# DMA transposes for Q and x in place of TensorE transposes, with a reordered start, in a linear-attention plus ELU-MLP kernel

## The chip, the cores and the metric

One core of a Trainium2 chip. The time is the device time of one execution in microseconds (us); smaller is better. Each kernel was run several times, and a run is called fast or slow by its time and its granted TensorE clock; only fast runs enter the verdicts. PE is TensorE (PEld its weight loads), DVE VectorE, ACT ScalarE, POOL GpSimd, SP SyncE. "L360" is line 360 of the kernel in question; the changed kernel has other line numbers than the kernel before, so the same matmul is L318 in one and L347 in the other.

## The reference, cut to what matters

```python
# q, k, v: (8, 8, 576, 64) float32;  g_norm: (64,)
kv  = einsum('bhsd,bhse->bhde', k, v)            # 64x64 for each batch and head
out = einsum('bhsd,bhde->bhse', q, kv)
rms = sqrt(mean(out * out, axis=-1, keepdims=True) + 1e-06)
x   = (out / rms * g_norm)                       # then heads side by side: (4608, 512)
h   = x @ w_in                                   # w_in  (512, 2048)
g   = where(h > 0, h, exp(minimum(h, 0)) - 1)    # ELU
return (g @ w_out).astype(float32)               # w_out (2048, 512)
```

Of the kernel before, what the change touches and what calls it, by code (L numbers as in the profile page):

```python
# [9 lines left out]
BF16 = mybir.dt.bfloat16  # L10
AF = mybir.ActivationFunctionType
ALU = mybir.AluOpType
# [4 lines left out]
def kernel(  # L17
# [13 lines left out]
    nc = tc.nc  # L31
# [6 lines left out]
    J = 4  # L38
# [2 lines left out]
    KC = DM // P  # L41
    FC = DF // P
    NT = B + 1

    const = ctx.enter_context(tc.tile_pool(name="const", bufs=1))
    stage = ctx.enter_context(tc.tile_pool(name="stage", bufs=1))
# [61 lines left out]
    def fetch(b, eng=nc.sync):  # L108
        fetch_q(b, eng)
        for name, src in (("k", k), ("v", v)):  # L110
            out_, in_ = fetch_kv(name, src, b)
            eng.dma_start(out=out_, in_=in_)  # L112

    def load_w_in(s):
        cols = slice(s * 512, s * 512 + 512)
        nc.gpsimd.dma_start(
            out=w_in_sb[:, :, cols], in_=moe_w_in.rearrange("(c p) f -> p c f", p=P)[:, :, cols]
        )

    def load_w_out(s):  # L120
        fs = slice(4 * s, 4 * s + 4)
        nc.gpsimd.dma_start(
            out=w_out_sb[:, fs, :], in_=moe_w_out.rearrange("(c p) f -> p c f", p=P)[:, fs, :]
        )
# [56 lines left out]
    def se_mm(T, j, qT, se_ps):  # L181

        ov = se_ps.rearrange("p (u l s e) -> p u l s e", u=2, l=2, s=2)
        for p in range(NPAIR):
            s, u = p // 2, p % 2
            if T < B:
                nc.tensor.matmul(  # L187
                    ov[:, u, :, s, :],
                    lhsT=qT[:, p, j * P : j * P + P],
                    rhs=bd_kv[:, T, p, :],  # L190
                    start=True,
                    stop=True,
                )
            else:
                for l in range(2):
                    nc.tensor.matmul(
                        ov[l * 64 : l * 64 + 64, u, :, s, :],
                        lhsT=qT[:, p, j * P + l * 64 : j * P + l * 64 + 64],
                        rhs=bd_kv[:, 2 * j + l, p, :],
                        start=True,  # L200
                        stop=True,
                    )
# [25 lines left out]
    def attention(T):  # L228
        st = {}

        def kv():
            if T == B:
                return
            kv_ps = at_tile(FP32)
            for u in range(2):
                kv_mm(T, [kv_ps[:, 0:512], kv_ps[:, 512:1024]], u)
            kv_v = kv_ps.rearrange("p (s x e) -> p s x e", s=2, e=P)[:, :, 0:2, :]
            bd_v = bd_kv[:, T].rearrange("p (s u) e -> p s u e", s=2)
            for l in range(2):
                ls = slice(l * 64, l * 64 + 64)  # L240
                nc.scalar.copy(bd_v[ls, :, :, ls], kv_v[ls, :, :, ls])

        def q_t():
            qt_ps = at_tile(BF16).rearrange("p (r t) -> p r t", r=NPAIR)
            for p in range(NPAIR):
                q_t_mm(bf["q", T], qt_ps, p)
            qT = attp.tile([P, NPAIR, G], BF16, name="qT", tag="qT")
            st["qT"] = qT
            nc.vector.tensor_copy(out=qT[:, 0:2, :], in_=qt_ps[:, 0:2, :])  # L249
            nc.scalar.copy(qT[:, 2:4, :], qt_ps[:, 2:4, :])  # L250

        def se(h):


            def product():
                se_ps = at_tile(FP32).rearrange("p (c f) -> p c f", c=2)
                for c in range(2):
                    se_mm(T, 2 * h + c, st["qT"], se_ps[:, c, :])
                st["se", h] = se_ps
                st["sq", h] = square(se_ps, 2)  # L260

            def sums():
                st["ss", h] = sum_heads(st.pop(("sq", h)), 2)

            def inv():
                inv_rms(st["ss", h])

            def scale():
                if h == 0:
                    st["xs"] = attp.tile([P, J, DM], BF16, name="xs", tag="xs")  # L270
                rows = st["xs"][:, 2 * h : 2 * h + 2, :]
                scale_rows(rows, st.pop(("se", h)), st.pop(("ss", h)), 2)

            return product, sums, inv, scale

        def x_t():
            xs = st["xs"]
            xt_ps = at_tile(BF16).rearrange("p (r t) -> p r t", r=NPAIR)
            for c in range(KC):
                for j in range(J):  # L280
                    nc.tensor.transpose(  # L281
                        xt_ps[:, c, j * P : j * P + P],
                        xs[:, j, c * P : c * P + P],
                        ident,
                    )
            x = attp.tile([P, KC, G], BF16, name="xT", tag="xT")
            xT[T] = x
            nc.vector.tensor_scalar(  # L288
                out=x[:, 0:2, :], in0=xt_ps[:, 0:2, :], scalar1=g_col, scalar2=None, op0=ALU.mult
            )  # L290
            nc.scalar.mul(x[:, 2:4, :], xt_ps[:, 2:4, :], g_col)  # L291

        pieces = {"kv": kv, "q": q_t, "x": x_t}
        for h in range(2):
            for name, piece in zip(("se", "sum", "inv", "mul"), se(h)):
                pieces[f"{name}{h}"] = piece
        return pieces
# [4 lines left out]
    def mm1(T, i, cols=(slice(0, 512),), relu=False, spare=False):  # L302
# [11 lines left out]
        for cs in cols:  # L314
            for a in range(2):
                f = 2 * i + a
                for c in range(KC):
                    nc.tensor.matmul(  # L318
                        h_ps[a][:, cs],
                        lhsT=w_in_sb[:, c, f * P : f * P + P],  # L320
                        rhs=x[:, c, cs],
                        start=(c == 0),
                        stop=(c == KC - 1),
                    )
# [49 lines left out]
    def mm2_half(T, i):  # L374
        mm2(T, i // 2, 8 * (i % 2), 8 * (i % 2) + 8)
# [82 lines left out]
    se_at = at_tile(FP32)  # L458
    se_ps += [se_at[:, 0:512], se_at[:, 512:1024]]
    for j in range(J):  # L460
        se_mm(0, j, qT0, se_ps[j])
    idle(10)
    xs0 = attp.tile([P, J, DM], BF16, name="xs", tag="xs")
    x0 = attp.tile([P, KC, G], BF16, name="xT", tag="xT")
    xT[0] = x0
    xt_ps = ps_m1.tile([P, 2, G], FP32, name="xt_ps", tag="mm1").rearrange(
        "p a t -> p (a t)"
    ).bitcast(BF16).rearrange("p (a r c t) -> p a r c t", a=2, r=2, c=KC)
# [47 lines left out]
            cast_kv("v", b, Q)  # L516

    fetch(1)
    for s in range(2):
        load_w_in(s)  # L520
    cast_q(1, Q)
    for s in range(2, 4):
        load_w_in(s)
    cast_kv("k", 1, Q)
    cast_kv("v", 1, Q)
    for s in range(4):
        load_w_out(s)

    def first_products(T, at, second, start, relu=(), spare=()):


        early, late = {}, {}
        for name, i in start.items():
            late.setdefault(i, []).append(name)
            if name in ("se0", "se1"):
                early.setdefault(i + 1, []).extend(("sum" + name[2], "inv" + name[2]))
                late.setdefault(i + 1, []).append("mul" + name[2])
        for i in range(9 if 8 in early else 8):
            if i == 8:
                for name in early[8] + late[8]:  # L540
                    at[name]()
                break
            cols = (slice(0, 256), slice(256, 512)) if T == 0 and i == 0 else (slice(0, 512),)
            rest = mm1(T, i, cols, i in relu, i in spare)
            for name in early.get(i, ()):
                at[name]()
            if i in second:
                second[i]()
            rest()
            for name in late.get(i, ()):  # L550
                at[name]()

    at = attention(1)
    at["fetch"] = lambda: fetch(2, nc.scalar)
    start = {"q": 1, "kv": 4, "se0": 5, "fetch": 6, "se1": 7}
    first_products(0, at, {}, start, (1, 3, 5, 7), (2, 5))
    mm2_half(0, 0)
    mm2_half(0, 1)
    at["x"]()
    mm2_half(0, 2)  # L560

    cast_all(2)
    fetch(3)
    at = attention(2)
    second = {i: (lambda i=i: mm2_quarter(0, 6 + i)) for i in range(8)}
    start = {"q": 1, "kv": 2, "se0": 3, "se1": 5, "x": 7}
    first_products(1, at, second, start, (1, 3, 5, 7))
    mm2_half(0, 7)

    for T in range(2, NT):  # L570
        second = {i: (lambda i=i: mm2_half(T - 1, i)) for i in range(8)}
        at, start = None, {}
        if T + 1 < NT:
            at, start = attention(T + 1), {"kv": 0, "q": 1, "se0": 2, "se1": 4, "x": 6}
            cast_all(T + 1)
        if T + 2 < B:
            fetch(T + 2)
        elif T + 2 == B:
            fetch_q(B)
        first_products(T, at, second, start)  # L580
    for i in range(8):
        mm2_half(NT - 1, i)

# [29 lines left out]
```

## The kernel before: the parts that the change and the argument touch

The 4608 tokens are worked in nine groups of 512. Groups 0 to 7 are the first 512 tokens of each batch, group 8 is the 64 left over from each. For a group the two MLP products are 64 matmuls each, 128x128 by 128x512. The attention of group T+1 is cut into small pieces, placed between the products of group T:

```python
def attention(T):
    def kv():                        # K^T V of the batch: 36 small matmuls, then two ScalarE copies
        ...
    def q_t():                       # Q must lie with head_dim on the partitions
        qt_ps = at_tile(BF16)...     # the one PSUM tile of the attention
        for p in range(NPAIR):
            q_t_mm(bf["q", T], qt_ps, p)                            # 16 TensorE transposes
        nc.vector.tensor_copy(out=qT[:, 0:2, :], in_=qt_ps[:, 0:2, :])
        nc.scalar.copy(qT[:, 2:4, :], qt_ps[:, 2:4, :])
    def se(h):                       # scores of half a group; square, sum, 1/rms, scale -> xs
        ...
    def x_t():                       # x must lie with d_model on the partitions
        for c in range(KC):
            for j in range(J):
                nc.tensor.transpose(xt_ps[:, c, j*P:j*P+P], xs[:, j, c*P:c*P+P], ident)
        nc.vector.tensor_scalar(out=x[:, 0:2, :], in0=xt_ps[:, 0:2, :], scalar1=g_col, ...)
        nc.scalar.mul(x[:, 2:4, :], xt_ps[:, 2:4, :], g_col)        # g_norm on the way out of PSUM
```

The steady loop, and the start (the attention of group 0 is done alone first, up to about 22 us):

```python
    fetch(1)                                   # Q, K, V of batch 1, SyncE
    for s in range(2):    load_w_in(s)         # weights: GpSimd, cast to bf16 on the way
    cast_q(1, Q)                               # GpSimd, waits for Q of batch 1
    for s in range(2, 4): load_w_in(s)
    cast_kv("k", 1, Q); cast_kv("v", 1, Q)
    for s in range(4):    load_w_out(s)
    ...
    at["fetch"] = lambda: fetch(2, nc.scalar)  # batch 2: issued by ScalarE inside group 0
    start = {"q": 1, "kv": 4, "se0": 5, "fetch": 6, "se1": 7}
    ...
    for T in range(2, NT):
        second = {i: (lambda i=i: mm2_half(T - 1, i)) for i in range(8)}
        if T + 1 < NT:
            at, start = attention(T + 1), {"kv": 0, "q": 1, "se0": 2, "se1": 4, "x": 6}
            cast_all(T + 1)
        if T + 2 < B: fetch(T + 2)
        ...
        first_products(T, at, second, start)
```

`first_products` issues eight steps; step i is an eighth of group T's first product, its ELU, an eighth of group T-1's second product, and the pieces whose number in `start` is i. A tuple such as (1, 3, 5, 7) after `start` names its Relu steps: there ScalarE also writes relu(h) to SBUF, and VectorE's last ELU operation, which then need not read PSUM, takes 0.69 us and not 1.22 in the start.

## Time and profile before

| | before |
|---|---|
| time, median of 4 runs | 320.69 us (320.2 to 321.54) |
| span of the profiled run | 317.4 us |
| PE busy | 299.1 us (94%) |
| first product of group 2 starts | 81.94 us |
| period of a steady group | 31.52 us |

The profiled run took 319.24 us; it is a fast run, but not one of the four, and it is 1.45 us below their median.

The chain of waits runs back from the last instruction; its line by engine, from the page of the kernel before:

```profile
PE 80%; DMA 8%; DVE 4%; ACT 4%; ACTq 1%; POOL 0%; issue 0%; SPq 0%; DVEq 0%
```

The windows view of the kernel before, over two steady groups. Columns: the stretch; its length and PE busy time with the number of instructions; then PEld, DVE, ACT, POOL; granted clock; DMA share; GB/s.

```profile
117.10:148.60 31.50, 31.50 (x213) 16.12 (x212) 19.47 (x23) 16.05 (x22) 7.97 (x14) 1.00 0.41 142
148.60:180.10 31.50, 31.50 (x213) 16.13 (x212) 20.17 (x23) 16.05 (x22) 8.12 (x14) 1.00 0.40 142
```

PE is busy for the whole of each stretch at full clock, while VectorE and ScalarE have a third to a half of it free. So in the steady part only PE's own work counts. Its timeline (start, length, engine, line, what) shows what that work costs:

```profile
153.18 1.06 PE L175 MATMUL at<-ident,q_bf 128*128 128x128 bf16 x16
154.07 1.89 PE L318 MATMUL h_ps<-xT,w_in_sb 128*128 128x512 bf16 x8
155.80 1.89 PE L360 MATMUL o_ps<-w_out_sb,gT 128*128 128x512 bf16 x8
...
172.23 1.06 PE L281 MATMUL at<-ident,xs 128*128 128x128 bf16 x16
173.12 1.89 PE L318 MATMUL h_ps<-xT,w_in_sb 128*128 128x512 bf16 x8
```

Read such lines from start to start, since a matmul's end overlaps the next one: the Q transposes hold PE from 153.18 to 154.07, 0.89 us, and the x transposes 0.89 us.

The start is different. The same view of the kernel before (in brackets: idle time before, and what ended it):

```profile
42.80 0.77 PE L187 MATMUL at<-bd_kv,qT 128*128 128x128 bf16 x8 [2.73 <-DVE xs L221]
43.36 4.32 PE L360 MATMUL o_ps<-w_out_sb,gT 128*128 128x512 bf16 x12
48.48 1.02 PE L360 MATMUL o_ps<-w_out_sb,gT 128*128 128x512 bf16 x4 [0.80 <-DMA w_out_sb<-in_moe_w_out_dram]
51.20 1.05 PE L281 MATMUL at<-ident,xs 128*128 128x128 bf16 x16 [1.70 <-DVE xs L221]
```

PE waits here, so here the order of loads and of other engines' work decides. (Where `xs`, the scaled scores, ended the wait, PE waited for VectorE to read the one PSUM tile of the attention, or for what it wrote.)

### The profile page before, as it was taken

The page shows a single profiled execution, that of the slowest core. Times are in us where ns is not written, and L with a number is a line of the kernel's source. Part 1 is how long each engine was busy: PE and PEld are TensorE (multiplying, and loading weights), DVE is VectorE, ACT ScalarE, POOL GpSimd, SP SyncE. Part 2 cuts the span into 40 slices and gives each one's busy share as a digit, 9 for nine tenths or more (in the row PEclk, how much of TensorE's full clock was granted, in tenths as well). Part 3 has the DMA queues.
Part 4 walks back from the last instruction along what each step waited for, and adds up shares of the span by engine and source line. Part 5 has one row for each costly group of instructions (what it writes and reads, how often), then busy time and mean ns, then how long its engine had stood idle before and what let it go on. Part 6 is the DMA issues. An engine that isn't in the chain of part 4 may idle for free.

```text
span 317.4 us, 4742 instructions
## 1 busy us (share of the span) xinstructions
PE 299.1 (94%) x1941; PEld 150.4 (47%) x1941; DVE 179.3 (56%) x217; ACT 156.5 (49%) x218; POOL 66.3 (21%) x117
## 2 busy tenths in 40 slices
PE   8778966998999999999999999999999999999993
PEld 3444523553554545454545454545454545444441
DVE  4565744578448744774487458745774676554400
ACT  3556933667445454545554555445544555334220
POOL 0246405950045005400540063002000000000000
PEclk9999979999999999999999999999999999999999
DMA  7999799920491049105810591034101010101122
GB/s 256 316 290 253 121 238 387 363 99 2 138 355 71 0 148 348 69 0 168 328 67 2 158 340 66 0 108 94 68 0 66 2 66 2 66 0 66 68 66 66
DMA packets 28565, 42.24 MB, mean 133 GB/s; under 512 B 5504, under 2 KB 17792, under 8 KB 28544
## 3 DMA queue, kind: packets, MB, share of 16 engines
q1 hardware_dynamic: 22208, 34.35, 31.4%
q0 software_dynamic: 4224, 4.19, 8.1%
q10 hardware_dynamic: 2112, 3.41, 3.0%
q8 instruction: 15, 0.25, 0.3%
q14 instruction: 6, 0.05, 0.0%
HBM read 36.70 MB, written 9.44 MB: 145 GB/s over the span
## 4 chain that ended last, share of the span: by engine, by line
PE 80%; DMA 8%; DVE 4%; ACT 4%; ACTq 1%; POOL 0%; issue 0%; SPq 0%; DVEq 0%
PE o_ps L360 36%; PE h_ps L318 35%; DMA w_in_sb<-in_moe_w_in_dram 5%; PE at L165 2%; PE at L281 2%; DMA st_v<-in_v_dram 2%; PE at L175 2%; PE at L187 2%; ACT elu_e L327 1%; DVE gT L344 1%; DVE ss L211 1%; ACTq L112 1%; DVE xs L221 1%; ACT elu_h L331 1%; ACT sq L206 1%; DVE elu_e L336 1%
## 5 line engine op out<-in xcount | busy, mean ns | idle before, releaser
L360 PE MATMUL o_ps<-w_out_sb,gT 128*128 128x512 bf16 x576 | 137.0, 382 | 0.8 <-DMA w_out_sb<-in_moe_w_out_dram 0.8
L318 PE MATMUL h_ps<-xT,w_in_sb 128*128 128x512 bf16 (+1 forms) x584 | 135.6, 376 | 1.7 <-DMA w_in_sb<-in_moe_w_in_dram 1.7
L327 ACT ACTIVATE elu_e<-h_ps 128x1024 bf16<-128x1024 f32 (+1 forms) x74 | 74.0, 1001 | 67.2 <-PE h_ps L318 62.6
L360 PEld LDWEIGHTS <-gT 128*128 128x128 bf16 x576 | 56.7, 99 | 69.3 <-issue 3.2
L336 DVE TENSOR_SCALAR elu_e<-elu_e 128x1024 bf16<-128x1024 bf16 (+1 forms) x73 | 35.6, 487 | 94.1 <-ACT elu_e L327 94.1
L318 PEld LDWEIGHTS <-w_in_sb 128*128 128x128 bf16 x584 | 55.2, 98 | 61.4 <-DMA w_in_sb<-in_moe_w_in_dram 2.2
L344 DVE TENSOR_TENSOR gT<-elu_e,h_ps 128x1024 bf16<-128x1024 bf16 (+1 forms) x65 | 78.3, 1205 | 6.8
L130 POOL CAST q_bf<-st_q 128x512 bf16<-128x512 f32 x32 | 19.3, 640 | 136.1 <-DMA st_q<-in_q_dram 92.3
L370 ACT COPY o_sb<-o_ps 128x512 f32<-128x512 f32 x36 | 21.1, 586 | 24.9 <-PE o_ps L360 24.9
L206 ACT ACTIVATE sq<-at 128x1024 bf16<-128x1024 f32 (+1 forms) x18 | 17.5, 981 | 13.7 <-PE at L187 11.1
L130 POOL CAST v_bf<-st_v 128x512 bf16<-128x512 f32 (+1 forms) x36 | 20.8, 620 | 12.5 <-DMA st_v<-in_v_dram 12.0
L211 DVE TENSOR_REDUCE ss<-sq 128x16 f32<-128x1024 bf16 x16 | 19.5, 1219 | 4.8 <-ACT sq L206 4.5
L130 POOL CAST k_bf<-st_k 128x512 bf16<-128x512 f32 (+1 forms) x35 | 19.6, 604 | 7.8 <-DMA st_k<-in_k_dram 7.8
L221 DVE TENSOR_TENSOR xs<-at,ss 128x1024 bf16<-128x1024 f32 x16 | 19.5, 1218 | 0.6 <-ACT ss L218 0.6
L291 ACT ACTIVATE xT<-at,g_col 128x1024 bf16<-128x1024 bf16 x8 | 8.9, 1114 | 19.0 <-DVE xT L288 19.0
L421 PE MATMUL idle_ps<-zeros,ident 128*128 128x512 bf16 x45 | 13.3, 434 | 1.4 <-POOL ident masks.py:199 1.4
L250 ACT COPY qT<-at 128x1024 bf16<-128x1024 bf16 x8 | 8.1, 1012 | 9.4 <-DVE qT L249 9.4
L187 PE MATMUL at<-bd_kv,qT 128*128 128x128 bf16 x120 | 9.3, 221 | 3.3 <-DVE xs L221 3.3
L187 PEld LDWEIGHTS <-qT 128*128 128x128 bf16 x128 | 8.5, 98 | 7.2 <-issue 3.9
L165 PE MATMUL at<-v_bf,k_bf 64*128 64x128 bf16 x288 | 9.8, 216 | 2.0 <-DVE v_bf L130 1.1
L165 PEld LDWEIGHTS <-k_bf 64*128 64x128 bf16 x288 | 8.3, 94 | 5.9 <-issue 4.8
L281 PE MATMUL at<-ident,xs 128*128 128x128 bf16 x128 | 8.4, 219 | 2.3 <-DVE xs L221 2.3
(46 smaller groups left out, 105.3 us busy)
## 6 DMA issues: line engine op xcount, KB each, us to landing
out_dram<-o_sb SPq DMA_DIRECT2D x16, 512.0 KB, 2.6
st_q<-in_q_dram SPq DMA_DIRECT2D x14, 512.0 KB, 5.5
st_k<-in_k_dram SPq DMA_DIRECT2D x6, 1152.0 KB, 8.7
st_v<-in_v_dram SPq DMA_DIRECT2D x6, 1152.0 KB, 10.9
w_in_sb<-in_moe_w_in_dram POOLq DMA_DIRECT2D x4, 512.0 KB, 13.0
w_out_sb<-in_moe_w_out_dram POOLq DMA_DIRECT2D x4, 512.0 KB, 9.4
st_k<-in_k_dram SPq DMA_DIRECT2D x2, 576.0 KB, 6.8
st_v<-in_v_dram SPq DMA_DIRECT2D x2, 576.0 KB, 7.8
```

The source lines that it names most:

```text
L130: eng.tensor_copy(out=out_, in_=in_)
L165: nc.tensor.matmul(kv_ps[s][:, u * P : u * P + P], lhsT=bf["k", T][rows, j, 2 * u : 2 * u + 2, :], rhs=bf["v", T][rows, j, 2 * u : 2 * u + ...
L187: nc.tensor.matmul(ov[:, u, :, s, :], lhsT=qT[:, p, j * P : j * P + P], rhs=bd_kv[:, T, p, :], start=True, stop=True,)
L206: nc.scalar.activation(sq, se_ps, AF.Square)
L211: nc.vector.reduce_sum(out=ss, in_=sq.rearrange("p c (h e) -> p (c h) e", h=H), axis=AX.X)
L221: nc.vector.tensor_tensor(out=xs.rearrange("p c (h e) -> p (c h) e", h=H), in0=se_ps.rearrange("p c (h e) -> p (c h) e", h=H), in1=ss.to_b ...
L318: nc.tensor.matmul(h_ps[a][:, cs], lhsT=w_in_sb[:, c, f * P : f * P + P], rhs=x[:, c, cs], start=(c == 0), stop=(c == KC - 1),)
L327: nc.scalar.activation(e[:, lo:hi, :], ps, AF.Exp)
L336: nc.vector.tensor_scalar(out=e[:, lo:hi, :], in0=e[:, lo:hi, :], scalar1=1.0, scalar2=1.0, op0=ALU.min, op1=ALU.subtract,)
L344: nc.vector.tensor_tensor(out=gT[T][:, 2 * i + lo : 2 * i + hi, :], in0=e[:, lo:hi, :], in1=h, op=ALU.add if relu else ALU.max,)
L360: nc.tensor.matmul(o_ps[T, j], lhsT=gT[T][:, f, j * P : j * P + P], rhs=w_out_sb[:, f, :], start=(f == 0), stop=(f == FC - 1),)
L370: nc.scalar.copy(o_sb[T][:, j % 2, :], o_ps.pop((T, j)))
```

## The change

Its intent: Q (from group 2) and x (from group 3) are transposed by DMA from SBUF to SBUF, so PE and the PSUM copies are spared; g_norm, which used to ride on the copy out of PSUM, is applied in place by VectorE. At the start, weight loads are queued early, and batch 2 goes from ScalarE's queue to SyncE's, held back by a tiny "gate" DMA that reads the last part of group 0's gT. The casts of Q, K and V move one group ahead, since Q must be in bf16 before its transpose goes out, and the score pieces move a step earlier. Cut to its core:

```diff
+        def q_dma():
+            qT = attp.tile([P, J, NPAIR, P], BF16, name="qT", tag="qT")
+            st["qT"] = lambda p, j: qT[:, j, p, :]
+            nc.sync.dma_start_transpose(
+                out=qT.rearrange("p j r t -> p (j r) t"),
+                in_=bf["q", T].rearrange("p j h d -> p (j h d)"),
+            )
...
+        def x_dma(h):
+            def turn():                                   # half a group: 256 KB
+                ...
+                nc.sync.dma_start_transpose(out=st["x"][:, js]..., in_=st["xs"][:, js, :]...)
+            def scale():
+                x = st["x"][:, 2 * h : 2 * h + 2]
+                nc.vector.tensor_scalar(out=x, in0=x, scalar1=g_col, scalar2=None, op0=ALU.mult)
...
     fetch(1)
-    for s in range(2):
+    for s in range(4):
         load_w_in(s)
     cast_q(1, Q)
-    for s in range(2, 4):
-        load_w_in(s)
+    for s in range(4):
+        load_w_out(s)
     cast_kv("k", 1, Q)
     cast_kv("v", 1, Q)
-    for s in range(4):
-        load_w_out(s)
...
+    def hold_loads():
+        gate = const.tile([1, 64], BF16, name="gate")
+        nc.sync.dma_start(out=gate, in_=gT[0][0:1, FC - 1, 0:64])
...
-    at["fetch"] = lambda: fetch(2, nc.scalar)
-    start = {"q": 1, "kv": 4, "se0": 5, "fetch": 6, "se1": 7}
-    first_products(0, at, {}, start, (1, 3, 5, 7), (2, 5))
-    mm2_half(0, 0)
-    mm2_half(0, 1)
+    start = {"q": 1, "kv": 4, "se0": 5, "se1": 7}
+    first_products(0, at, {}, start, (2, 3, 6), (2, 5))
+    hold_loads()
+    fetch(2)
+    cast_all(2)
+    for i in range(5):
+        mm2_quarter(0, i)
     at["x"]()
...
-            at, start = attention(T + 1), {"kv": 0, "q": 1, "se0": 2, "se1": 4, "x": 6}
+            start = {"kv": 0, "se0": 1, "xd0": 2, "se1": 3, "xd1": 4, "xg0": 5, "xg1": 6}
...
+        if T + 2 < NT:
+            ahead["qd"]()          # Q of the group after the next, at the end of the step loop
```

More of the change, by code (lines that the diff above doesn't have):

```diff
@@ L43 @@
     NT = B + 1
+    Q_BY_DMA, X_BY_DMA = 2, 3
     const = ctx.enter_context(tc.tile_pool(name="const", bufs=1))
@@ L188, in se_mm @@
                     ov[:, u, :, s, :],
-                    lhsT=qT[:, p, j * P : j * P + P],
+                    lhsT=qT(p, j),
                     rhs=bd_kv[:, T, p, :],
@@ L197, in se_mm @@
                         ov[l * 64 : l * 64 + 64, u, :, s, :],
-                        lhsT=qT[:, p, j * P + l * 64 : j * P + l * 64 + 64],
+                        lhsT=qT(p, j)[:, l * 64 : l * 64 + 64],
                         rhs=bd_kv[:, 2 * j + l, p, :],
@@ L247, in q_t @@
             qT = attp.tile([P, NPAIR, G], BF16, name="qT", tag="qT")
-            st["qT"] = qT
+            st["qT"] = lambda p, j: qT[:, p, j * P : j * P + P]
             nc.vector.tensor_copy(out=qT[:, 0:2, :], in_=qt_ps[:, 0:2, :])
             nc.scalar.copy(qT[:, 2:4, :], qt_ps[:, 2:4, :])
+        def q_dma():
[5 more added lines that the diff above has]
+            )
         def se(h):
@@ L286, in x_t @@
             x = attp.tile([P, KC, G], BF16, name="xT", tag="xT")
-            xT[T] = x
+            xT[T] = lambda c, cs: x[:, c, cs]
             nc.vector.tensor_scalar(
@@ L291, in x_t @@
             nc.scalar.mul(x[:, 2:4, :], xt_ps[:, 2:4, :], g_col)
-        pieces = {"kv": kv, "q": q_t, "x": x_t}
+        def x_dma(h):
+            def turn():
+                if h == 0:
+                    st["x"] = attp.tile([P, J, KC, P], BF16, name="xT", tag="xT")
+                    xT[T] = lambda c, cs: st["x"][:, :, c, :]
+                js = slice(2 * h, 2 * h + 2)
+                nc.sync.dma_start_transpose(
+                    out=st["x"][:, js].rearrange("p j c t -> p (j c) t"),
+                    in_=st["xs"][:, js, :].rearrange("p j f -> p (j f)"),
+                )
+            def scale():
+                x = st["x"][:, 2 * h : 2 * h + 2]
+                nc.vector.tensor_scalar(out=x, in0=x, scalar1=g_col, scalar2=None, op0=ALU.mult)
+            return turn, scale
+        pieces = {"kv": kv, "q": q_t, "x": x_t, "qd": q_dma}
+        for h in range(2):
+            pieces[f"xd{h}"], pieces[f"xg{h}"] = x_dma(h)
         for h in range(2):
@@ L320, in mm1 @@
                         lhsT=w_in_sb[:, c, f * P : f * P + P],
-                        rhs=x[:, c, cs],
+                        rhs=x(c, cs),
                         start=(c == 0),
@@ L460 @@
     for j in range(J):
-        se_mm(0, j, qT0, se_ps[j])
+        se_mm(0, j, lambda p, j: qT0[:, p, j * P : j * P + P], se_ps[j])
     idle(10)
@@ L464 @@
     x0 = attp.tile([P, KC, G], BF16, name="xT", tag="xT")
-    xT[0] = x0
+    xT[0] = lambda c, cs: x0[:, c, cs]
     xt_ps = ps_m1.tile([P, 2, G], FP32, name="xt_ps", tag="mm1").rearrange(
@@ L533, in first_products @@
         for name, i in start.items():
-            late.setdefault(i, []).append(name)
             if name in ("se0", "se1"):
                 early.setdefault(i + 1, []).extend(("sum" + name[2], "inv" + name[2]))
-                late.setdefault(i + 1, []).append("mul" + name[2])
+                late.setdefault(i + 1, []).insert(0, "mul" + name[2])
+            late.setdefault(i, []).append(name)
         for i in range(9 if 8 in early else 8):
@@ L551, in first_products @@
                 at[name]()
+    def hold_loads():
+        gate = const.tile([1, 64], BF16, name="gate")
+        nc.sync.dma_start(out=gate, in_=gT[0][0:1, FC - 1, 0:64])
     at = attention(1)
-    at["fetch"] = lambda: fetch(2, nc.scalar)
-    start = {"q": 1, "kv": 4, "se0": 5, "fetch": 6, "se1": 7}
-    first_products(0, at, {}, start, (1, 3, 5, 7), (2, 5))
-    mm2_half(0, 0)
-    mm2_half(0, 1)
+    start = {"q": 1, "kv": 4, "se0": 5, "se1": 7}
[5 more added lines that the diff above has]
+        mm2_quarter(0, i)
     at["x"]()
-    mm2_half(0, 2)
-    cast_all(2)
+    mm2_quarter(0, 5)
+    ahead = attention(2)
+    ahead["qd"]()
     fetch(3)
-    at = attention(2)
-    second = {i: (lambda i=i: mm2_quarter(0, 6 + i)) for i in range(8)}
-    start = {"q": 1, "kv": 2, "se0": 3, "se1": 5, "x": 7}
-    first_products(1, at, second, start, (1, 3, 5, 7))
-    mm2_half(0, 7)
+    cast_all(3)
+    at, ahead = ahead, attention(3)
+    quarters = iter(range(6, 16))
+    counts = (0, 1, 1, 1, 2, 1, 1, 1)
+    second = {
+        i: (lambda n=n: [mm2_quarter(0, next(quarters)) for _ in range(n)])
+        for i, n in enumerate(counts)
+    }
+    start = {"kv": 2, "se0": 3, "se1": 5, "x": 7}
+    first_products(1, at, second, start, (1, 3, 4, 6))
+    for i in quarters:
+        mm2_quarter(0, i)
+    ahead["qd"]()
     for T in range(2, NT):
         second = {i: (lambda i=i: mm2_half(T - 1, i)) for i in range(8)}
-        at, start = None, {}
+        at, start = ahead, {}
         if T + 1 < NT:
-            at, start = attention(T + 1), {"kv": 0, "q": 1, "se0": 2, "se1": 4, "x": 6}
-            cast_all(T + 1)
-        if T + 2 < B:
-            fetch(T + 2)
-        elif T + 2 == B:
-            fetch_q(B)
+            start = {"kv": 0, "se0": 1, "xd0": 2, "se1": 3, "xd1": 4, "xg0": 5, "xg1": 6}
+        if T + 2 < NT:
+            fetch(T + 2) if T + 2 < B else fetch_q(B)
+            cast_all(T + 2)
+            ahead = attention(T + 2)
         first_products(T, at, second, start)
+        if T + 2 < NT:
+            ahead["qd"]()
     for i in range(8):
```

## The prediction

> **What bounds the kernel now.** From about 80 us on, TensorE. In the windows table each stretch of one group (118 to 150, 150 to 181, 181 to 213 us) is 31.5 us long with PE busy throughout at granted clock 1.00; the chain of waits is 80% PE. VectorE (about 19.8 us of 31.5) and ScalarE (16.0) have room. The timeline of 149 to 182 us prices the pieces: eight 512-column matmuls 1.73 us (128 in a group: 27.7), the 16 Q transposes 0.89 us, the 16 x transposes 0.89. Before 82 us PE has holes: 1.17 us on w_in (27.9), 2.73 us before the second score piece (42.8; ScalarE was issuing DMAs, one for 3.10 us), 0.80 us on w_out (48.5), 1.70 us (51.2), three smaller.
>
> **What the change does.**
> 1. PE transposes go: Q for groups 2 to 8 (7 x 0.89), x for 3 to 8 (6 x 0.89): 11.6 us, all on the critical path. Period 31.5 to about 29.7 us.
> 2. Their PSUM copies go: per group 1.4 us VectorE, 2.1 us ScalarE. The g scaling returns as two in-place 128x1024 bf16 operations; the elu operation of that shape takes 0.43 us, 0.86 while GpSimd casts. Off the path.
> 3. DMA transposes come, on SyncE: Q 512 KB, x in two of 256 KB. The trace has none. A plain 512 KB store lands in 2.6 us. The Trainium skill, "DMA: Bandwidth & Descriptors", Latency and other measured facts, gives 261 GB/s for a non-contiguous transpose: estimate, with latency and per-tile issue, 4 to 7 us for Q, 3 to 5 for an x half. No run here shows it yet. Windows, estimated from the timeline: Q goes out at a group's start and is needed about 7.5 us later; x half 0 has about 9 us; x half 1 about 6 us before VectorE scales it, 7 before PE waits. It should just fit; x half 1 and Q are the tight ones.
> 4. Start: w_out is queued some 13 us earlier (before: 32.5 us); ScalarE no longer issues batch 2 (about 4.7 us on the chain). The holes at 42.8 to 51.2 us should mostly close, so group 1 starts near 48 instead of 53.8 us. The w_in wait stays. But batch 2, held until group 0's gT is complete (about 44 us), lands as late as before (V cast until about 58), and its KV product now comes earlier: PE waits there up to 4 us. Net gain about 4 to 5 us.
>
> **Sum.** 320.8 - 11.6 - 4.5 = 304.7; plus about 1.5 us for stalls on late transposes: 306 us. Range 301 to 314. Faster by over 2%: 0.78; within 2%: 0.17; slower: 0.05.
>
> **What would show it.** Lines: PE transposes of q_bf fall from 144 to 32. Windows: groups 3 to 7 take about 29.7 us, PE still 100% busy. DMA issues: transposes land under 7 us. Waits: nothing over 0.5 us a group on qT or xT. Start: the hole before the second score piece under 1.5 us, group 2's KV product waiting for v_bf 1 to 4 us.
>
> **What would make it wrong.** A DMA transpose over 8 us (few engines, or SyncE's queue held by it), so that each group waits for Q or x: 2 us a group would eat the steady gain. Large stores or loads ahead of a transpose in its queue. Transposes slowing batch loads so casts come late. The granted clock falling as matmuls get denser.

## The result, and the profile after

| | before | after |
|---|---|---|
| time, median of 4 runs | 320.69 us | 305.38 us (305.13 to 306.45) |
| span of the profiled run | 317.4 us | 303.4 us |
| KV product of group 3 starts | 85.56 us | 81.92 us |
| period of a steady group (KV product to KV product) | 31.52 us | 29.73 us |

The ratio is 0.9526 (95% interval 0.9496 to 0.9556). Here and below a ratio is the mean time of one kernel's fast runs over that of the kernel before in the same rounds, so not quite the ratio of the medians. Two changed versions from different sets of rounds are compared through these ratios; the experiments below ran in three sets, on three chips.

The windows view of the changed kernel, two steady groups:

```profile
111.70:141.40 29.70, 29.54 (x179) 14.32 (x182) 18.97 (x23) 13.94 (x20) 8.02 (x14) 1.00 0.66 186
141.40:171.10 29.70, 29.54 (x178) 14.35 (x180) 18.91 (x23) 13.94 (x20) 8.16 (x14) 1.00 0.62 186
```

PE is still busy all the time, but the stretch is 1.8 us shorter. ScalarE lost 2.1 us of work and VectorE 0.5 to 1.3; the DMA engines' share rose from 0.41 to some 0.64. Where the transposes went, in the view of DMA issues (count, median us from issue to landing) of the changed kernel:

```profile
xT<-xs SPq DMA_TRANSPOSE x12, 3.1
qT<-q_bf SPq DMA_TRANSPOSE x7, 5.1
```

The timelines of SP and then of PE in the changed kernel show how they fit in time:

```profile
139.11 3.28 SPq L257 DMA_TRANSPOSE qT<-q_bf  x1
142.45 1.14 SPq L85 DMA_DIRECT2D st_q<-in_q_dram  x2
...
152.44 1.25 SPq L309 DMA_TRANSPOSE xT<-xs  x1
154.13 0.36 SPq L411 DMA_DIRECT2D out_dram<-o_sb  x1
159.67 1.23 SPq L309 DMA_TRANSPOSE xT<-xs  x1
```

```profile
141.40 1.18 PE L167 MATMUL at<-v_bf,k_bf 64*128 64x128 bf16 x36
...
145.97 0.61 PE L189 MATMUL at<-bd_kv,qT 128*128 128x128 bf16 x8
...
171.13 1.18 PE L167 MATMUL at<-v_bf,k_bf 64*128 64x128 bf16 x36
```

From KV product to KV product is the period, 29.73 us. Q is issued at 139.11; 5.0 us later, at 144.1, it is there; PE uses it at 145.97. The margin is about 1.8 us here. It is not so in every group: for groups 3 to 8 the Q transposes landed in 5.0, 5.1, 5.0, 6.0, 6.7 and 5.0 us, and were needed 6.8 us after their issue (5.75 in group 8). So the margin was 1.8 us at best, and in group 7 a weight load of PE already waited:

```profile
205.35 0.52 PEld L189 LDWEIGHTS <-qT 128*128 128x128 bf16 x8 [0.24 <-DMA qT<-q_bf]
```

What made two of them land later was not traced. SyncE itself is held 3.3 us by this one instruction. The second half of x, issued at 159.67, lands near 162.8 us; VectorE's in-place g scaling of it starts at 165.33 and takes 0.48 us, without waiting.

The start after the change, the lines that answer to those shown of before:

```profile
42.03 0.61 PE L189 MATMUL at<-bd_kv,qT 128*128 128x128 bf16 x8 [2.33 <-DVE xs L223]
42.48 6.17 PE L389 MATMUL o_ps<-w_out_sb,gT 128*128 128x512 bf16 x19
48.48 1.06 PE L291 MATMUL at<-ident,xs 128*128 128x128 bf16 x16
```

The hole before the second score piece is still there (2.33 us after 2.73). The waits at 48.5 and 51.2 us are gone. The timelines of VectorE and ScalarE in the kernel before show why ScalarE's DMA issue made the later wait and not the hole:

```profile
40.42 0.98 ACTq L83 DMA_DIRECT2D st_q<-in_q_dram  x2
41.53 1.22 DVE L221 TENSOR_TENSOR xs<-at,ss 128x1024 bf16<-128x1024 f32 x1
42.05 3.10 ACTq L112 DMA_DIRECT2D st_v<-in_v_dram  x1
47.02 1.03 ACT L206 ACTIVATE sq<-at 128x1024 bf16<-128x1024 f32 x1
```

The hole ended when VectorE had written this `xs`, at 42.75 us. VectorE had worked without a break since 38.74 us, and ScalarE had finished its part (1/rms, at 40.54 us) as its issuing began. What the issuing held up was the squares of the second score piece: they ran at 47.02 us, and at 42.67 in the changed kernel; the x transposes moved from 51.20 to 48.48 us. After the hole the twenty second-product matmuls between 42.48 and 48.48 us (19 have a record) took 300 ns each from start to start, not the 216 of the steady part. The windows view of the changed kernel tells why; the last three columns are clock, DMA share, GB/s:

```profile
42.00:44.00 2.00, 1.97 (x12) 1.00 (x12) 1.80 (x3) 1.02 (x1) 0.00 (x0) 0.63 0.22 37
44.00:46.00 2.00, 2.00 (x6) 0.76 (x5) 1.38 (x2) 0.52 (x2) 0.00 (x0) 0.52 0.25 20
46.00:48.00 2.00, 1.95 (x10) 0.88 (x9) 0.80 (x1) 0.18 (x1) 0.00 (x0) 1.00 0.86 298
```

After the hole the granted clock is about half for some 3 us, and PE counts as nearly 100% busy in it. This is not new: in the kernel before the clock in 42 to 48 us was 0.78, 0.50 and 0.87, and the first twelve second-product matmuls took 4.32 us. The DMA engines are nearly idle in 42 to 46 us: w_out is in (its last slice landed at 43.4), and batch 2, held until 44.4, has barely started.

Adding up the spans: 3.6 us of the gain are there by group 3's KV product (85.56 to 81.92 us), the other 10.4 us of the 14.0 come in the six groups' attention after it, against 6 x 1.78 = 10.7 us of removed PE work. The medians differ by 15.3 us, not 14.0, because the profiled run of the kernel before is quicker than its median; where its other runs lose this 1.45 us no kept trace shows, so the 3.6 us for the start is rather a lower figure.

### The profile page after: what moved, and what is told of

It is laid out like the page before. It is cut to its first block, busy times and chain, and to the rows that moved or that the text cites. A ratio compares the mean times of both kernels' runs of the same rounds, so it can differ in the third digit from the quotient of the medians.

```text
span 303.4 us, 4351 instructions
## 1 busy us (share of the span) xinstructions
PE 285.6 (94%) x1703; PEld 138.6 (46%) x1733; DVE 174.5 (58%) x216; ACT 141.9 (47%) x204; POOL 67.7 (22%) x117
## 4 chain that ended last, share of the span: by engine, by line
PE 79%; DMA 11%; DVE 2%; ACT 2%; POOL 2%; SPq 1%; issue 1%; POOLq 0%; DVEq 0%
PE h_ps L347 38%; PE o_ps L389 37%; DMA w_in_sb<-in_moe_w_in_dram 6%; DMA st_v<-in_v_dram 5%; PE at L167 2%; PE at L189 2%; POOL v_bf L132 1%; DVE gT L373 1%; DVE xs L223 1%; ACT elu_e L356 1%; SPq L85 1%; PE at L198 0%; DVE elu_e L365 0%; ACT xT L301 0%; ACT elu_h L360 0%
## 5 line engine op out<-in xcount | busy, mean ns | idle before, releaser
L389 PE MATMUL o_ps<-w_out_sb,gT 128*128 128x512 bf16 x556 | 134.3, 383 | 1.0
L347 PEld LDWEIGHTS <-w_in_sb 128*128 128x128 bf16 x584 | 55.7, 98 | 65.8 <-issue 2.2
L373 DVE TENSOR_TENSOR gT<-elu_e,h_ps 128x1024 bf16<-128x1024 bf16 (+1 forms) x66 | 79.5, 1205 | 6.9
L365 DVE TENSOR_SCALAR elu_e<-elu_e 128x1024 bf16<-128x1024 bf16 (+1 forms) x73 | 33.0, 452 | 82.0 <-ACT elu_e L356 81.9
L132 POOL CAST q_bf<-st_q 128x512 bf16<-128x512 f32 x32 | 20.0, 663 | 130.4 <-DMA st_q<-in_q_dram 130.4
L132 POOL CAST v_bf<-st_v 128x512 bf16<-128x512 f32 (+1 forms) x36 | 20.7, 617 | 11.6 <-DMA st_v<-in_v_dram 11.2
L213 DVE TENSOR_REDUCE ss<-sq 128x16 f32<-128x1024 bf16 x16 | 19.5, 1218 | 5.3 <-ACT sq L208 5.1
L132 POOL CAST k_bf<-st_k 128x512 bf16<-128x512 f32 (+1 forms) x35 | 20.4, 625 | 5.4 <-DMA st_k<-in_k_dram 4.6
L223 DVE TENSOR_TENSOR xs<-at,ss 128x1024 bf16<-128x1024 f32 x16 | 19.5, 1218 | 0.6 <-ACT ss L220 0.6
L243 ACT CAST bd_kv<-at 64x256 bf16<-64x256 f32 x14 | 5.2, 369 | 9.9 <-PE at L167 9.8
L373 DVE TENSOR_TENSOR gT<-elu_e,elu_h 128x1024 bf16<-128x1024 bf16 x7 | 6.0, 861 | 2.9 <-ACT elu_h L360 2.8
L360 ACT ACTIVATE elu_h<-h_ps 128x1024 bf16<-128x1024 f32 (+1 forms) x8 | 7.3, 926 | 0.0
## 6 DMA issues: line engine op xcount, KB each, us to landing
w_out_sb<-in_moe_w_out_dram POOLq DMA_DIRECT2D x4, 512.0 KB, 19.5
```

The source lines that it names most:

```text
L132: eng.tensor_copy(out=out_, in_=in_)
L213: nc.vector.reduce_sum(out=ss, in_=sq.rearrange("p c (h e) -> p (c h) e", h=H), axis=AX.X)
L223: nc.vector.tensor_tensor(out=xs.rearrange("p c (h e) -> p (c h) e", h=H), in0=se_ps.rearrange("p c (h e) -> p (c h) e", h=H), in1=ss.to_b ...
L347: nc.tensor.matmul(h_ps[a][:, cs], lhsT=w_in_sb[:, c, f * P : f * P + P], rhs=x(c, cs), start=(c == 0), stop=(c == KC - 1),)
L365: nc.vector.tensor_scalar(out=e[:, lo:hi, :], in0=e[:, lo:hi, :], scalar1=1.0, scalar2=1.0, op0=ALU.min, op1=ALU.subtract,)
L373: nc.vector.tensor_tensor(out=gT[T][:, 2 * i + lo : 2 * i + hi, :], in0=e[:, lo:hi, :], in1=h, op=ALU.add if relu else ALU.max,)
```

## The experiments

Twelve kernels ran, all correct. Unless stated, each is the changed kernel with one edit, and its reported runs are fast ones. After each median stands its ratio to the kernel before; a ratio higher by 0.003 is about 1 us more.

### Is it PE's time for the transposes? One back, the other back, both back

Q of groups 3 to 8 on PE again, in the place of the DMA issue:

```diff
-            ahead["qd"]()
+            ahead["q"]()
```

> Changed kernel, but Q of groups 3 to 8 is transposed by TensorE again (at the end of the group before, in the place of the DMA issue), x stays with DMA. If the steady gain is the PE time of the transposes, it loses 6 x 0.89 = 5.3 us: about 310.7 us, with a steady period of 30.6 us instead of 29.73. Rival: the gain came from the relief of VectorE and ScalarE (PSUM copies) or of the one PSUM tile; then the loss is not a multiple of 0.89 us a group.

Measured: 311.58 us, ratio 0.9733. The period in its trace is 30.63 us.

x of groups 3 to 8 on PE again:

```diff
-            start = {"kv": 0, "se0": 1, "xd0": 2, "se1": 3, "xd1": 4, "xg0": 5, "xg1": 6}
+            start = {"kv": 0, "se0": 1, "se1": 3, "x": 6}
```

> Changed kernel, but x of groups 3 to 8 is transposed by TensorE with its PSUM copies on VectorE and ScalarE, Q stays with DMA. PE-time theory: again 6 x 0.89 = 5.3 us lost, about 310.7 us, period 30.6 us. Rival (copies or waits matter): a loss clearly different from that of Q, since x has other copies and comes at the end of the group.

Measured: 311.36 us, ratio 0.9740; in its trace the x transposes of three groups in a row are 30.74 and 30.63 us apart.

Both edits together:

> Changed kernel with Q and x of groups 3 to 8 both transposed by TensorE; the new start stays. If the two DMA moves add up: 305.4 + 6.2 + 6.0 = 317.6 us by the single runs, 316.1 by PE time alone (2 x 5.3), with a period of 31.5 us as in the kernel before. If more than that, the shared PSUM tile (KV, Q, scores, x) makes new waits; if less, the single runs each paid something only once.

Measured: 316.81 us, ratio 0.9863; period 31.52 us, as in the kernel before:

```profile
115.30 1.18 PE L167 MATMUL at<-v_bf,k_bf 64*128 64x128 bf16 x36
146.82 1.18 PE L167 MATMUL at<-v_bf,k_bf 64*128 64x128 bf16 x36
```

What follows: each of the two moves is worth 0.9 us in every period, in the periods they add, and both are worth 0.9863 - 0.9526 = 0.0337 of 321 us, 10.8 us, which is the 12 x 0.89 us of PE time. The rival is that relief of VectorE or ScalarE brought the gain. That Q and x cost the same says little against it, because their copies are nearly alike (0.68 and 1.01 us for Q, 0.75 and 1.11 for x). What speaks against it is that the waits view lists no wait of PE's matmuls, for any engine, from group 3's KV product to the end of the steady groups in the kernel before, the changed kernel and this run: where PE never waits for another engine, relief of that engine cannot shorten the period. A kernel that keeps the transposes on PE and drops only the copies was not run.

In their whole times the single runs lost more than 5.3 us (6.0 to 6.2 by their medians, 6.6 to 6.9 by their ratios), so these add less well than the periods. With Q on PE, 0.7 us of it is a new wait in group 1, where the Q transposes wait for the PSUM tile that x still holds. With x on PE, group 3's KV product came 0.25 us later, and group 8 waited for its Q, which still came by DMA:

```profile
239.62 0.64 PE L198 MATMUL at<-bd_kv,qT 128*64 128x128 bf16 x16 [0.51 <-DMA qT<-q_bf]
```

### How much margin do the DMA transposes have?

From group 3 on, n useless transposes of 256 KB are issued ahead of each Q transpose (n = 1 and 3):

```diff
             st["qT"] = lambda p, j: qT[:, j, p, :]
+            if T > 2:
+                for _ in range(n):
+                    scrap = attp.tile([P, 8, P], BF16, name="scrap", tag="scrap", bufs=n)
+                    nc.sync.dma_start_transpose(out=scrap,
+                        in_=bf["q", T].rearrange("p j h d -> p (j h d)")[:, 0:1024])
```

> Changed kernel; from group 3 on, one useless 256 KB DMA transpose of half of Q is issued on SyncE ahead of the real one. It holds the queue some 1.3 us. In the trace Q lands at about 5.1 us after its issue and is first needed 6.9 us after it (139.1, 144.2, 146.0 us), so 1.8 us are to spare: no change, 305.4 us, under 0.5 us a group of PE waiting on qT. If the margin is thinner than read (or fetches behind it matter): more than 306.5 us.

Measured: 308.5 us, ratio 0.9612: about 2.8 us slower, where none was expected. The trace splits it. Of the 5.0 us that its profiled span is longer (it is the slowest of its four runs), 2.9 are there at group 3's KV product and come from before the first useless transpose (issued at 82.5 us; a product of PE at 81.67 us is already that late): in this run K and V of batch 2 were cast 1.4 and 1.6 us later, PE waited for V, and the clock went to 0.50 afterwards. Why this start came out slower is open. The rest is the edit: PE waited for qT in three of the six groups,

```profile
120.22 0.62 PE L189 MATMUL at<-bd_kv,qT 128*128 128x128 bf16 x8 [0.96 <-DMA qT<-q_bf]
...
209.91 0.62 PE L189 MATMUL at<-bd_kv,qT 128*128 128x128 bf16 x8 [0.30 <-DMA qT<-q_bf]
```

and 0.43 us in group 8. So the margin is about 1.8 us in a group where the transpose lands in 5.0 us, but landing varied from 4.6 to 6.4 us in this run, and a delay of 1.6 us on the queue sometimes shows. The expectation failed because it took the margin from one group and the median; the changed kernel's own trace had a group with none.

> The same with three useless transposes ahead of each Q: the real one is issued some 3.8 us later, so it lands 2.0 us after TensorE needs it. If the reading of the margin is right, PE waits about 2 us in each of six groups: about 317 us, the steady period near 31.7 us. Rival: Q transposes are far from the path (the order on SyncE hides it), then no more than 306.5 us.

Measured: its two fast runs took 323.48 and 325.88 us, where 317 was expected; ratio 1.0106 (1.0054 to 1.0158): about 1% slower than the kernel before. Two more runs, the profiled one among them, are slow, so its length is not used; but it shows where the time goes:

```profile
PE at L189 <- DMA qT<-q_bf: 11.3, 5, 2.9
PE at L198 <- DMA qT<-q_bf: 3.0, 1, 3.0
```

That is 14.3 us of waiting in six groups (us in total, times, longest), near the 12 expected. And a wait of 2 us costs more than 2 us, as its PE timeline shows after one of them:

```profile
90.14 0.62 PE L189 MATMUL at<-bd_kv,qT 128*128 128x128 bf16 x8 [2.04 <-DMA qT<-q_bf]
90.59 2.95 PE L353 MATMUL h_ps<-xT,w_in_sb 128*128 128x512 bf16 x8
93.33 2.56 PE L395 MATMUL o_ps<-w_out_sb,gT 128*128 128x512 bf16 x8
95.73 1.89 PE L353 MATMUL h_ps<-xT,w_in_sb 128*128 128x512 bf16 x8
```

The eight matmuls that take 1.73 us from start to start take 2.74 and 2.40 after the wait; the granted clock was 0.50 in 92 to 94 us. This trace is of a slow run, but the mean clock of the two fast ones was low too (0.980 and 0.981, against 0.989 to 0.995 for the changed kernel). So the transposes are free only as long as they are in time; 4.1 to 5.4 us of delay on the queue (I had expected 3.8) turn the whole gain into a loss.

### What in the new start is worth something?

The start of the kernel before under the new steady part (old order of weights and casts, batch 2 on ScalarE in step 6, old Relu steps in group 0, no hold; group 1 keeps its new schedule). The core of the edit:

```diff
-    start = {"q": 1, "kv": 4, "se0": 5, "se1": 7}
-    first_products(0, at, {}, start, (2, 3, 6), (2, 5))
-    hold_loads()
-    fetch(2)
+    at["fetch"] = lambda: fetch(2, nc.scalar)
+    start = {"q": 1, "kv": 4, "se0": 5, "fetch": 6, "se1": 7}
+    first_products(0, at, {}, start, (1, 3, 5, 7), (2, 5))
```

> Changed kernel with the start of the kernel before (w_in and w_out queued between the casts, batch 2 issued by ScalarE in group 0, the old places of the Relu form, no hold); DMA transposes kept. The two traces say that group 2's first product moved from 81.9 to 78.0 us: so it should lose about 4 us, about 309.4 us. Rival: the start gains nothing by itself, because without the removed Q transposes of group 2 the holes are the same; then 305 to 306 us.

Measured: 308.73 us, ratio 0.9642, so about 3.7 us lost; its four runs spread from 306.48 to 310.58 us, more than any other's, and that spread was not explained.

Only the order of weight loads and casts as before:

> Changed kernel, only the order of weight loads and casts as before (w_in slices 2 and 3 after the Q cast, w_out after all casts of batch 1); hold and SyncE issue kept. If the early queueing of w_out carries the gain at the start: w_out then lands near 46 us or later, and TensorE waits for it in the first second products: 2 to 4 us lost, 307.5 to 309.5 us. If taking batch 2 off ScalarE carries it: under 1 us lost.

Measured: 305.98 us, ratio 0.9561: about 1 us lost, not clear of noise (95% intervals 0.9527 to 0.9595 and, for the changed kernel, 0.9496 to 0.9556). Queueing w_out 13 us earlier is worth little, because w_out, queued at 31.7 us, still landed in time (its last slice at 46.8 us, and at 48.4 in the kernel before, where batch 2 ran beside it): no PE wait for w_out is left in this trace. The rest of the start's gain, 0.9642 - 0.9561 = 0.0081 or 2.6 us, with a similar uncertainty, lies in what the two kernels do not share: batch 2's issue and hold, the Relu steps and the order of the quarters. These were not separated further.

The gate DMA taken away, batch 2 on SyncE as soon as its buffers are free:

```diff
-    hold_loads()
     fetch(2)
```

> Changed kernel without the gate DMA: batch 2 is issued on SyncE as soon as its staging buffers are free (about 32 us), beside the w_out loads. If the hold protects w_out: w_out lands some 4 to 8 us later, TensorE waits for it in the first second products, 1 to 4 us lost. If the hold only delays batch 2: V of batch 2 is cast some 5 us or more earlier, but TensorE got to its KV product at 58.6 us, only 0.6 us before the cast ended, so under 1 us gained.

Measured: 315.34 us, ratio 0.9852: 10.5 us lost, the largest effect of any edit to the start. PE's timeline:

```profile
46.74 1.02 PE L389 MATMUL o_ps<-w_out_sb,gT 128*128 128x512 bf16 x4 [2.32 <-DMA w_out_sb<-in_moe_w_out_dram]
51.71 1.44 PE L389 MATMUL o_ps<-w_out_sb,gT 128*128 128x512 bf16 x3 [3.95 <-DMA w_out_sb<-in_moe_w_out_dram]
54.98 3.55 PE L389 MATMUL o_ps<-w_out_sb,gT 128*128 128x512 bf16 x8 [1.83 <-DMA w_out_sb<-in_moe_w_out_dram]
```

The four w_out slices landed 21.5 to 33.3 us after their issue, instead of 16.5 to 22.1; PE waited 8.1 us for them, and the clock stayed at 0.50 from 50 to 58 us. The direction was expected, the size was not (1 to 4 us): the expectation left out that Q of batch 2 went out at 19.5 us and K at 27.3, not at 32, so that nearly all of w_out shared the engines, and it left out the clock. It left out a third thing: with batch 2 earlier, the Q transpose of group 2 too went out earlier, beside the loads (41.25 us, and 52.35 in the changed kernel). SyncE's timeline:

```profile
41.25 8.81 SPq L257 DMA_TRANSPOSE qT<-q_bf  x1
```

It landed only after 15.0 us, and in 48 to 56 us, while the last two slices of w_out were still to come, the DMA engines moved 184 to 239 GB/s, after some 300 in 40 to 48. How much of the loss is due to the loads of batch 2 and how much to this transpose was not separated. The run also shows what the issue on ScalarE had been doing in the kernel before: it held batch 2 back to 40 us.

### Two chains that end together at group 2's KV product

Three edits: the gate reads an earlier part of gT; two quarters of the second product go into PE's hole; both.

```diff
-        nc.sync.dma_start(out=gate, in_=gT[0][0:1, FC - 1, 0:64])
+        nc.sync.dma_start(out=gate, in_=gT[0][0:1, FC - 5, 0:64])      # hold_early
...
-    first_products(0, at, {}, start, (2, 3, 6), (2, 5))
+    first_products(0, at, {7: lambda: [mm2_quarter(0, n) for n in (0, 1)]},
+                   start, (2, 3, 6), (2, 5))                           # fill
```

> Changed kernel, the gate reads the part of gT that product 5 writes (38.6 us) and not that of product 7 (43.6 us), so batch 2 is issued about 5 us earlier, when w_out is nearly in (the DMA engines stood nearly idle from 42 to 46 us). Theory: two chains end at group 2's KV product almost together, PE's own (58.6 us) and the cast of V (59.2 us); moving one alone gains under 0.8 us: 304.6 to 305.4 us. Rival: the V load was the bound (it is 5% of the chain of waits), then 3 to 5 us gained.

Measured: 304.05 us, ratio 0.9499 (0.9465 to 0.9534): about 0.9 us gained by the ratio, a little more than the expected 0.8, but not clear of noise. V of batch 2 was cast by 55.7 us, PE came at 58.4 us and did not wait.

> Changed kernel, the first two quarters of group 0's second product are put into the hole of TensorE before the second score piece (2.33 us at 39.7 to 42.0). PE work 1.7 us moves into the hole, and the granted clock, which fell to 0.52 to 0.63 in 42 to 46 us after the hole, may stay high. But V of batch 2 still comes at 59.2 us, so under 0.8 us gained: 304.6 to 305.4 us. Rival: PE's own chain alone was the bound, then 1.7 to 3.4 us gained. If w_out's first half is not in by 40 us, PE waits for it instead.

Measured: 305.64 us, ratio 0.9548: nothing gained. PE was 1.4 us earlier at the KV product, and lost it there:

```profile
57.69 0.29 PE L167 MATMUL at<-v_bf,k_bf 64*128 64x128 bf16 x4 [0.21 <-POOL v_bf L132]
58.44 0.29 PE L167 MATMUL at<-v_bf,k_bf 64*128 64x128 bf16 x4 [0.46 <-POOL v_bf L132]
58.99 1.08 PE L167 MATMUL at<-v_bf,k_bf 64*128 64x128 bf16 x24 [0.27 <-POOL v_bf L132]
```

> Both together: the hole filled and batch 2 issued 5 us earlier. Two-chain theory: now both ends of group 2's KV product move, 1.7 us from the fill plus up to 1.7 us if the clock stays at 1.00: 302 to 303.7 us, more than the sum of the two alone. Rival (only one of the chains was the bound): no more than the better of the two.

Measured: 303.52 us (303.49 to 304.05, six runs), ratio 0.9481: the best ratio among these three, below both single edits. The KV product starts at 57.36 us without a wait. Against the changed kernel this is 0.9526 - 0.9481 = 0.0045, some 1.4 us; the two 95% intervals (0.9446 to 0.9517 and 0.9496 to 0.9556) still overlap a little and the rounds are not shared, so read it as about half a per cent. Against the early gate alone, in the same rounds, it is 0.5 us by the medians, within that run's spread (303.42 to 305.15). It beats the kernel before by over 5%. The pattern of the times (nothing, a little, more than either) is what two chains of nearly the same length give, but the times alone do not prove it; the traces do more: of these three, PE waits for V only with the fill alone, and not where V comes earlier.

### Is it the hole that lowers the clock?

The early gate, and nine useless matmuls in the hole instead of useful ones:

```diff
+    def keep_busy():
+        t = ps_m2.tile([P, DM], FP32, name="busy_ps", tag="mm2")
+        for _ in range(9):
+            nc.tensor.matmul(t, lhsT=ident, rhs=zeros, start=True, stop=True)
-    first_products(0, at, {}, start, (2, 3, 6), (2, 5))
+    first_products(0, at, {7: keep_busy}, start, (2, 3, 6), (2, 5))
```

> The early gate, plus nine useless 512-column matmuls in the hole before the second score piece (1.9 us), instead of useful work. If the hole is what lowers the granted clock (0.63 and 0.52 in 42 to 46 us with the early gate, 1.00 with the hole filled with useful work), the clock stays at 1.00 in 42 to 46 us and the first second products take 216 ns each again; the x transposes then wait for VectorE, so about 1.2 us gained over the early gate: 302.8 to 303.6 us. Rival: the fall has another cause, then the clock falls as before and the time is that of the early gate, 304.1 us.

Measured: 303.83 us, ratio 0.9454, just above the expected time (other rounds, on another chip, than the early gate's 304.05 us and 0.9499, so the size of the gain is only roughly known). The windows view of this kernel:

```profile
42.00:44.00 2.00, 1.47 (x13) 0.84 (x12) 1.90 (x3) 0.63 (x1) 0.00 (x0) 1.00 1.10 332
44.00:46.00 2.00, 2.00 (x11) 0.91 (x10) 1.55 (x2) 0.70 (x2) 0.00 (x0) 1.00 1.09 389
```

With the hole filled the clock stays at 1.00, and the twenty second-product matmuls take 4.4 us (43.17 to 47.55) instead of 6.0. Group 1's first product starts at 49.45 us, against 50.21 with the early gate alone. In all three kernels that fill the hole, with useful work or not, the clock stays at 1.00 in 42 to 46 us. Of the eleven profiled kernels that leave it open (2.2 to 2.7 us), eight fall to 0.50 to 0.52 (one of them in a slow run). So PE's idleness is what brings the fall here. It does not always: with Q on PE, with one useless transpose and without the hold the hole was 2.2 to 2.3 us too, and the clock stayed at 1.00 up to 48 us. What decides it was not found.

## Why the prediction was right, point by point

The time, 306 us predicted and 305.38 measured, was right, and so was its main term.

1. **PE transposes, 11.6 us on the critical path, period 29.7 us.** Right: the period is 29.73 us, PE is still busy throughout, and putting the transposes back one by one and together gives 0.9 us a period each. Shown by three runs.
2. **PSUM copies off the path.** Right as far as the traces tell: in the steady groups PE waits for no other engine, before or after. The in-place g scaling takes 0.48 us each time.
3. **DMA transposes, 4 to 7 us for Q and 3 to 5 for an x half, windows just large enough.** Right: 5.1 and 3.1 us by the median (5.0 to 6.7 and 3.0 to 4.1). Q was the tight one: needed 6.8 us after its issue and not 7.5, with 1.8 us to spare at best and 0.1 in group 7. Not foreseen in size: SyncE is held 3.3 us by each Q transpose. The 1.5 us set aside for late transposes was too much; the only wait on a DMA transpose that the changed kernel's trace has for PE is one weight load that waited 0.2 us for qT.
4. **Start, 4 to 5 us, on top of group 2's Q.** This is the term that was mis-sized, and its steps were partly wrong. Up to group 3's KV product 3.6 us were gained, with the 0.89 us of group 2's Q in it, so about 2.7 us for the start itself by the spans; undoing the start cost 3.7 us, give or take 2. So 0.8 to 1.8 us less than the 4.5 that were summed, if the forecast of 4 to 5 was missed at all.
   - "The hole before the second score piece under 1.5 us": wrong, 2.33 us. I had blamed ScalarE's DMA issue, but that began only when ScalarE's work for the hole was done; VectorE ended the hole before, and ends it now, busy without a break from 34.8 to 43.6 us. What the DMA issue had caused was the 1.70 us at 51.2 (1.55 us of it come back in the run with the old start).
   - "Group 1 starts near 48": wrong, 50.38 us. The hole is followed by a granted clock of half, which I had not costed though the trace before showed it; it stretched twenty matmuls from 4.3 to 6.0 us.
   - "PE waits 1 to 4 us for v_bf": wrong, under 0.5 us, because PE came later than I thought, at 58.56 us, as the V cast was ending (59.18).
   - "w_out queued 13 us earlier": true but worth only about 1 us; what protects w_out is that batch 2, and with it the Q transpose of group 2, is held back.

The two errors, 1.5 us too much for stalls and some 0.8 to 1.8 us too much for the gain at the start, have opposite signs and nearly cancelled: that the sum came out closer than its parts was luck.

## What to carry to other kernels

Where one engine is busy without a gap, the worth of a move off it is its own start-to-start time in the trace, once per group, as long as the work that replaces it lands in time; measure that margin by delaying it on purpose, and look at its worst case and not at its median (here 1.8 us at best and 0.1 in one group). In a start-up phase, find every chain that ends at the same instruction before you shorten one of them, and check which loads must not run beside each other: taking away the hold of one batch cost ten times what queueing the weights late did. And count a PE hole of 2 us as more than 2 us when the clock column drops after it.

## What the Trainium skill lacked or had wrong

- "TensorE: Matmul & The Clock Gate", Why this matters for your kernels, says to keep idle gaps of PE below about 3 us. Here holes of 2.04 to 2.73 us were already followed by a clock near 0.5 for about 3 us (2.04 us with the clock at 0.50 from 92 to 94 us in the run with three useless transposes, a slow run; 2.33 us with 0.52 in the changed kernel, a fast one), though not every time (2.2 us in the run with Q on PE: 1.00).
- "DMA: Bandwidth & Descriptors", Latency and other measured facts, gives a bandwidth for transposes, 261 GB/s, but for sizes like these neither a time to landing nor how long the issuing queue is held. The runs show, from SBUF to SBUF, beside batch loads and by the median: 512 KB lands in 5.1 us (103 GB/s from issue to landing, so well below that bandwidth) and holds SyncE 3.3 us; 256 KB lands in 3.1 us and holds it 1.23 us.
- "VectorE: DVE Perf Modes", The three transpose paths, lists 390 ns for a 128x128 transpose on TensorE and 1309 ns by DMA. Here the record of one on PE is 219 ns long, but sixteen in a row took 0.89 us from start to start, 56 ns each, and 5.1 us by one DMA, 0.32 us each. The rule of the same page, Rules for kernel authors, to use TensorE where PSUM will do as a destination, leaves out which engine is full: here the slower path won, because PE had no gap and the DMA engines had.
